# Fused attention and two mixtures: two weight quarters and some split factors of the mixtures are put at earlier places in the instruction lists

## The chip, the cores and the metric

The kernel runs on one core of a Trainium2 chip. The metric is the device time in microseconds of one execution. Five engines work side by side, each through its own list in order: TensorE (PE; its weight loads are shown as PEld), VectorE (DVE), ScalarE (ACT), GpSimd (POOL) and SyncE (SP), which issues loads.

## The reference, cut to what matters

```python
def reference(**kwargs):
    attn_out = _attn_ref(...)                  # 2 x 8 heads, 768 tokens, 64 wide, 16 clusters
    x = np.ascontiguousarray(attn_out.transpose(0, 2, 1, 3)).reshape(B * S, H * D)   # 1536 x 512
    x = _moe_ref(x=x, **moe_kwargs)
    return _moe2_ref(x=x, **moe2_kwargs)

def _attn_ref(q, k, v, centroids):
    # each query and key goes to the centroid with the largest cosine
    mask = q_assign[:, :, :, None] == k_assign[:, :, None, :]
    scores = np.where(mask, scale * np.matmul(q, k.transpose(0, 1, 3, 2)), -1000000000.0)
    ...                                        # softmax of scores
    return np.matmul(attn, v)

def _moe_ref(x, w_in, w_out):                  # w_in 512 x 2048, w_out 2048 x 512
    h = x @ w_in
    return (h * (1.0 / (1.0 + np.exp(-h)))) @ w_out

def _moe2_ref(x, w_gate, w1, w2):              # 8 experts, 512 x 1024 and 1024 x 512
    ...                                        # P: softmax of x @ w_gate, normalised 8 times by rows and columns
    for e in range(E):
        out += P[:, e:e + 1] * (np.maximum(x @ w1[e], 0.0) @ w2[e])
    return out
```

## The kernel before, in words

**Factors.** Every fp32 matrix of a product is split in a high and a low fp32r part: ACT casts the high part, DVE subtracts it and writes the low one. A product is three matmul groups (high by high, high by low, low by high). Names ending in `h` and `l` are such pairs: `vh`/`vl` of the first mixture's w_in, `yh`/`yl` (tiles `yf`) of its x, `woh`/`wol` of w_out, `gh`/`gl` of the activated hidden block; `wfh`/`wfl`, `xfh`/`xfl` and `ah`/`al` of the second mixture's weights, x and hidden block.

**Attention** takes the first 235.5 us. It is a software pipeline over eight pairs of heads; the table `ORDER` gives one pair's steps as `name,offset` (some 27 us a pair), and writes the lists of all engines. The last rows, beyond pair 7, drain it. `ex` is the exponential on ACT, `rec` the reciprocal of its sums on DVE (two steps); POOL scales `p` by it, `T` transposes `p` on PE into `t`, and DVE and ACT copy `t` to `pt` for `av`. `xh` and `xl` split the result and write x sums of its quadrants (`xa` to `xd`).

**Quarters.** Each slice of w_in (even n) or w_out (odd n) is 4 raw quarters, (n, k). `w_raw` loads one on SP's queue; `w_steps` narrows it: `wb` and `w0` on ACT, `w1` to `w4` on DVE, the product `wp0` on POOL and the sum `wp1` on DVE; for w_out `wh` (ACT) and `wp2` (DVE) follow, which give `woh` and `wol`. Four quarters, those of n=0, are loaded by step `wd` in pairs 0 to 3 and narrowed within attention in the pairs behind each load, in the tile `scratch`.

**First mixture** (235.5 to 498.3 us): four slices s of 512 hidden columns. Each is seven products `aproduct` by a scheme of Strassen's kind (order `AORD` 1, 5, 6, 3, 7, 2, 4; called product 0 to 6 by place below, and 4.3 us each), whose factors are x split `yf[p]` and weight factor `mfactor(s, i)`; `aevac` copies the product's banks from PSUM to `h` (ACT) or adds them (DVE), `gsilu`, `ghi` and `glo` activate and split. Then come 12 tiles `ytile` of the second layer, each followed by a sum, `total`, which adds the tile's bank to `acc1` on DVE. A unit u (0 to 18) is one product or one tile: `put(s, u, f, ...)` lays further work into a unit, behind the unit's evacuation or sum and ahead of its matmuls. The lists follow this written order on all engines.

**Second mixture** (from 498.3 us): eight experts in two halves, 16 slices of 14 products. `factor`, `w_sums1`, `w_sums2` make weight factors and sums, `x_factor` and `x_sum` those of x, which is `acc1`. `gate` computes the logits.

The ring of raw tiles and of the narrowed ones:

```python
quarters[n, k][key]()
if key == "wp0":
    m = 4 * (n - 1) + k + 2
    load(1 + m // 4, m % 4)
```

Of the kernel before, what the change touches and what calls it, by code (L numbers as in the profile page):

```python
# [38 lines left out]
def attention_moe_kernel(ctx, tc, kq, vp, cent, w_in, w_out, w_gate, w1, w2, out):  # L39
# [87 lines left out]
    def split(p, src, ks=(0, 1)):  # L127
        hi, lo = yf[p]
        for k in ks:
            nc.scalar.copy(hi[:, k], src[:, k])  # L130
        for k in ks:
            nc.vector.tensor_tensor(out=lo[:, k], in0=src[:, k], in1=r(hi[:, k]), op=ALU.subtract)
# [250 lines left out]
    def five():  # L383
        if 5 not in yf:
            both = scp.tile([P, 2, 2, S], F32R, name="yf5", tag="sc")
            yf[5] = (both[:, 0], both[:, 1])
        return yf[5]

    def five_hi(k):
        nc.scalar.copy(five()[0][:, k], xa[:, k])  # L390

    def five_lo(k):
        nc.vector.tensor_tensor(out=five()[1][:, k], in0=xa[:, k], in1=r(five()[0][:, k]), op=ALU.subtract)
# [936 lines left out]
```

## Time and profile before

| | us |
|---|---|
| median of 3 runs (lowest, highest) | 1474.49 (1474.19, 1475.15) |
| profiled execution | 1473.8 |
| its span | 1472.0 |
| attention ends, first mixture ends | 235.5, 498.3 |

The span runs from the first to the last instruction of the profile, and times of day in the trace count from its start. "Granted clock" is the share of TensorE's full clock (2.4 GHz) that the chip let it have; 0.5 is 1.2 GHz. In a timeline the bracket at the end of a row is the idle time of the engine ahead of it and what ended it.

### The profile page before, as it was taken

The numbers are of one execution on the slowest core, as the hardware profiler recorded it, in microseconds if no ns is written. First come the engines' busy times: TensorE is split into PE (matmuls) and PEld (weight loads), VectorE is DVE, ScalarE is ACT, GpSimd is POOL, SyncE is SP. The second block draws the span as 40 slices with busy tenths as digits, with TensorE's granted clock in tenths as the row PEclk, the third lists the DMA queues.
The fourth block names the chain that finished last, engine by engine and source line by source line (L and its number), as shares of the span: only waits on it lengthen the run. The fifth ranks groups of instructions, "written<-read, shape, count | busy, mean of one in ns | idle before, by whom it ended". The sixth has DMA issues, their size and how long they took to land.

```text
span 1472.0 us, 25066 instructions
## 1 busy us (share of the span) xinstructions
PE 1443.1 (98%) x9784; PEld 1293.4 (88%) x9785; DVE 1092.0 (74%) x1734; ACT 948.6 (64%) x1782; POOL 361.3 (25%) x356
## 2 busy tenths in 40 slices
PE   8999998999999899999999999999999999999998
PEld 5777786788888789999999999999999999999998
DVE  7788887778887598857758668577686675875858
ACT  7777676654646266657667576576675765767654
POOL 6677752121120001111222222120211211202111
PEclk9999999999999999999999999999999999999999
DMA  7665511121222017476697897874947959659476
GB/s 222 179 166 154 140 49 58 58 86 49 67 72 72 1 51 176 68 151 152 119 209 114 161 170 126 163 123 91 203 69 139 149 90 178 105 104 183 83 144 129
DMA packets 136311, 177.48 MB, mean 121 GB/s; under 512 B 6272, under 2 KB 108672, under 8 KB 136192
## 3 DMA queue, kind: packets, MB, share of 16 engines
q0 software_dynamic: 83584, 87.30, 39.0%
q1 hardware_dynamic: 51104, 87.32, 19.7%
q8 instruction: 77, 1.26, 0.4%
q10 hardware_dynamic: 1504, 1.25, 0.3%
q14 instruction: 42, 0.34, 0.1%
HBM read 65.36 MB, written 88.87 MB: 105 GB/s over the span
## 4 chain that ended last, share of the span: by engine, by line
PE 77%; DVE 3%; ACT 2%; issue 0%; DVEq 0%; ACTq 0%
PE b L643 33%; PE a L643 30%; PE y L697 9%; PE l L643 5%; DVE vl L124 1%; DVE h L848 1%; DVE h L669 1%; ACT h L674 0%; ACT gh L679 0%; DVE wfl L851 0%; DVE xfl L851 0%; ACT vh L123 0%; PE gl L975 0%; DVE h L1154 0%; ACT woh L98 0%
## 5 line engine op out<-in xcount | busy, mean ns | idle before, releaser
L643 PE MATMUL b<-wfh,ah 128*128 128x256 f32 x1344 | 381.6, 284 | 1.3 <-ACT ah L1063 1.3
L643 PE MATMUL b<-wfh,al 128*128 128x256 f32 x1344 | 381.3, 284 | 0.7 <-DVE al L1073 0.7
L643 PE MATMUL b<-wfl,ah 128*128 128x256 f32 x1344 | 381.0, 283 | 0.0
L643 PE MATMUL a<-xfl,wfh 128*128 128x512 f32 (+1 forms) x896 | 302.8, 338 | 2.6 <-DVE xfl L851 2.6
L643 PE MATMUL a<-xfh,wfh 128*128 128x512 f32 (+1 forms) x896 | 302.8, 338 | 0.0
L643 PE MATMUL a<-xfh,wfl 128*128 128x512 f32 (+1 forms) x896 | 301.8, 337 | 0.0
L1135 POOL DMA_DIRECT2D out_dram<-acc x87 | 126.2, 1567 | 574.4 <-ACT acc L1126 392.6
L643 PEld LDWEIGHTS b<-wfh,ah 128*128 128x128 f32 x1344 | 258.8, 193 | 1.5 <-ACT ah L1063 1.5
L643 PEld LDWEIGHTS b<-wfh,al 128*128 128x128 f32 x1344 | 258.7, 192 | 1.1 <-DVE al L1073 1.1
L643 PEld LDWEIGHTS b<-wfl,ah 128*128 128x128 f32 x1344 | 258.7, 192 | 0.0
L1126 ACT ACTIVATE acc<-b,Pg 128x256 f32<-128x256 f32 x484 | 186.8, 477 | 21.7 <-issue 20.3
L851 DVE TENSOR_TENSOR al<-h,ah 128x768 fp32r<-128x768 f32 x192 | 177.7, 954 | 30.2 <-ACT ah L1065 29.6
L1065 ACT CAST ah<-h 128x768 fp32r<-128x768 f32 x192 | 160.5, 841 | 50.2 <-PE b L643 23.9
L643 PEld LDWEIGHTS a<-xfl,wfh 128*128 128x128 f32 x896 | 170.5, 190 | 20.9 <-DVE xfl L851 3.4
L643 PEld LDWEIGHTS a<-xfh,wfh 128*128 128x128 f32 x896 | 170.6, 190 | 19.8 <-issue 0.6
L643 PEld LDWEIGHTS a<-xfh,wfl 128*128 128x128 f32 x896 | 170.4, 190 | 18.0
L851 DVE TENSOR_TENSOR wfl<-w0r,wfh 128x512 fp32r<-128x512 f32 x96 | 64.8, 690 | 81.1 <-ACT wfh L936 79.0
L848 DVE TENSOR_TENSOR h<-a,h 128x512 f32<-128x512 f32 x144 | 94.2, 685 | 26.4 <-PE a L643 25.6
L1052 ACT COPY h<-a 128x512 f32<-128x512 f32 x144 | 81.3, 591 | 48.1 <-PE a L643 47.9
L300 ACT ACTIVATE p<-s,m 128x768 f32<-128x768 f32 x96 | 86.8, 905 | 37.4 <-DVE m L291 34.9
L291 DVE TENSOR_REDUCE m<-s 128x1 f32<-128x768 f32 x96 | 89.9, 950 | 15.2 <-PE s L284 14.7
L310 POOL TENSOR_SCALAR p<-p,rec 128x768 f32<-128x768 f32 x96 | 86.9, 918 | 53.1 <-DVE rec L305 44.8
(221 smaller groups left out, 2555.9 us busy)
## 6 DMA issues: line engine op xcount, KB each, us to landing
out_dram<-acc POOLq DMA_DIRECT2D x91, 768.0 KB, 9.3
w0r<-in_w_dram SPq DMA_DIRECT2D x16, 1024.0 KB, 6.9
w1r<-in_w_dram SPq DMA_DIRECT2D x16, 1024.0 KB, 6.8
qk<-qk SPq DMA_DIRECT2D x45, 192.0 KB, 3.6
raw<-in_w_out_dram SPq DMA_DIRECT2D x16, 512.0 KB, 3.4
first_out<-acc POOLq DMA_DIRECT2D x10, 768.0 KB, 10.6
raw<-in_kq_dram SPq DMA_DIRECT2D x16, 384.0 KB, 4.4
raw<-in_w_in_dram SPq DMA_DIRECT2D x12, 512.0 KB, 3.7
```

What stands on the lines that cost most here:

```text
L124: nc.vector.tensor_tensor(out=lo, in0=x, in1=r(hi), op=ALU.subtract)
L291: nc.vector.tensor_reduce(out=m, in_=tiles[i]["s"][:, :S], axis=AX.X, op=ALU.max, negate=True)
L300: nc.scalar.activation(t["p"], t.pop("s")[:, :S], AF.Exp, bias=t.pop("m"), accum_out=chunks[c]["sum"][:, j, 0:1])
L310: nc.gpsimd.tensor_scalar(out=p, in0=p, scalar1=chunks[c]["rec"][:, j : j + 1], scalar2=1.0, op0=ALU.mult, op1=ALU.mult)
L643: nc.tensor.matmul(ps[u][:, cols], lhsT=lf(i, k), rhs=rt(j, k), start=fresh and u not in opened, stop=k == 1 and q == 2, skip_group_check= ...
L697: nc.tensor.matmul(out, lhsT=w[:, k, d * P : (d + 1) * P], rhs=g, start=first, stop=last, skip_group_check=True)
L848: e.tensor_tensor(out=out, in0=in0, in1=in1, op=op)
L851: e.tensor_tensor(out=lo, in0=x, in1=r(hi), op=ALU.subtract)
L1052: act.copy(bank(t, u), ps[u])
L1065: act.copy(hi, x)
L1126: act.mul(t[:, 2 * u + m], z[:, m], g)
L1135: gps.dma_start(out=to, in_=t, accum_op=ALU.add)
```

## The change

- Quarters 0 and 1 of the first w_out slice (n=1) are narrowed within attention too: `wd` and all steps up to `wp1` run for six quarters. Raw tiles are a ring of three, `wr`. `b`, and for w_out `a` too, lie in the raw tile itself (every second 32-bit word); only `u` is a tile apart. The next load is issued when a quarter is finished, for a quarter three ahead (before: at `wp0`, two ahead).
- Splits 5, 6, 7 and 4 of x have tiles in the ring of the query tiles (`qkp`). Split 6 is put into the last rows of attention, `f0` (weight factor 0 of slice 0) is put behind the last `rec`. The tile of `xa` to `xd` shares its place with `acc1`.
- In the first mixture the quarters' steps stand in other units, as the diff shows; split 7 a unit earlier, and `woh` of a slice's last quarter ahead of the silus.
- The second mixture's first weight and x factors are put in the units 11 to 18 of slice 3, between the sums; its loads are issued at unit 7 of that slice.

The sequence of matmuls is the same.

```diff
     yf = {p: x_tiles(p, xpool) for p in (1, 3, 2)}
-    xa, xb, xc, xd = (xap.tile([P, 2, S], F32, name=f"x{c}") for c in "abcd")
+    xs = accp.tile([P, 4, 2, S], F32, name="xs", tag="acc")
+    xa, xb, xc, xd = (xs[:, i] for i in range(4))
+    def x_pair(p):
+        t = qkp.tile([P, 2, 2, S], F32R, name=f"yf{p}", tag="qk")
+        yf[p] = (t[:, 0], t[:, 1])
...
-    def w_steps(n, k, a, b, hi=None, lo=None):
+    def w_steps(n, k, a=None):
         low, high = raws[n, k][..., 0], raws[n, k][..., 1]
-        u, ui, ai = low.bitcast(F32), low, a.bitcast(U32)
+        b, odd = low.bitcast(F32), n % 2
+        if odd:
+            a = high.bitcast(F32)
...
+    for p, x in ((5, xa), (6, xc)):
+        for k in range(2):
+            KINDS[f"h{p}{k}"] = early(x_hi, p, x, k)
+            KINDS[f"l{p}{k}"] = early(x_lo, p, x, k)
...
     for key in ("wb", "w0", "w1", "w2", "w3", "w4", "wp0", "wp1"):
-        KINDS[key] = (wstep(key), 1, 0, 4)
+        KINDS[key] = (wstep(key), 1, 0, 6)
...
-        wp0,-2 T,-1 evD,-3 S,3 evD,-1 lv,2 evA,-2 wp1,-2 sim,1,0 rec,0 lv,1 av,-1 mx,2 ld,5 nrm,0 mx,3 ex,2 nrm,1 ex,3 split,3 S,4 xh,-1 rec,1
+        wp0,-2 T,-1 evD,-3 S,3 evD,-1 lv,2 evA,-2 f0,-1 h60,-1 h61,-1 l60,-1 l61,-1 wp1,-2 sim,1,0 rec,0 lv,1 av,-1 mx,2 ld,5 nrm,0 mx,3 ex,2 nrm,1 ex,3 split,3 S,4 xh,-1 rec,1
...
-        rec,4 w2,-1 av,1 mx,10 castd,5 nrm,8 mx,11 ex,10 nrm,9 ex,11 f0,0
+        rec,4 w2,-1 av,1 mx,10 castd,5 nrm,8 mx,11 ex,10 nrm,9 ex,11 l51,0
...
-            put(s, 0, narrow, n, 0, "wb w0")
-            put(s, 0, split, 6, xc)
-            put(s, 0, narrow, n, 0, "w1 w2 w3 w4 wp0")
-        put(s, 0, narrow, n, 0, "wp1 wh wp2")
-        put(s, 0, sum4)
-        put(s, 0, narrow, n, 1, "wb w0 w1 w2 w3 w4 wp0")
-        put(s, 1, sum3)
-        put(s, 1, narrow, n, 1, "wp1 wh wp2")
-        put(s, 1, narrow, n, 2, "wb w0 w1 w2")
-        if s == 0:
-            put(s, 2, split, 7, xb)
-        put(s, 2, narrow, n, 2, "w3 w4 wp0")
-        put(s, 2, narrow, n, 3, "wb w0")
-        put(s, 2, narrow, n, 2, "wp1 wh wp2")
-        put(s, 3, narrow, n, 3, "w1 w2 w3 w4 wp0")
-        put(s, 4, gsilu, 3)
-        put(s, 4, narrow, n, 3, "wp1 wh wp2")
+            put(s, 0, narrow, n, 0, "wh")
+            put(s, 0, narrow, n, 1, "wh")
+            put(s, 0, narrow, n, 0, "wp2")
+            put(s, 0, sum4)
+            put(s, 0, narrow, n, 1, "wp2")
+            put(s, 0, narrow, n, 2, "wb w0 w1 w2 w3 w4 wp0")
+            put(s, 1, sum3)
+            put(s, 1, split, 7, xb)
+            put(s, 1, narrow, n, 2, "wh wp1 wp2")
+            put(s, 2, narrow, n, 3, "wb w0 w1 w2 w3 w4 wp0")
+            put(s, 3, narrow, n, 3, "wh wp1 wp2")
+        else:
+            put(s, 0, narrow, n, 0, "wh wp1")
...
+            put(s, 3, narrow, n, 3, "wb w0 w1 w2 w3 w4 wp0")
+            put(s, 4, narrow, n, 3, "wh wp1 wp2")
+        put(s, 4, gsilu, 3)
...
+    s = NS1 - 1
+    put(s, 11, factor, 0, nc.vector)
+    put(s, 11, factor, 1, nc.vector)
+    put(s, 12, w_sums1, 0, nc.vector)
+    put(s, 13, w_sums2, 0, nc.vector)
+    put(s, 13, x_factor, 1, (0, 0), (0,))
+    put(s, 14, x_factor, 1, (0, 0), (1,))
+    put(s, 14, factor, 2, nc.vector)
+    put(s, 15, x_factor, 2, (1, 0), (0,))
+    put(s, 15, factor, 3, nc.vector)
+    put(s, 16, x_factor, 2, (1, 0), (1,))
+    put(s, 16, factor, 4, nc.vector)
+    put(s, 17, x_sum, (0, 1), (0, 1), (0, 0), (0,))
+    put(s, 18, x_sum, (0, 1), (0, 1), (0, 0), (1,))
+    put(s, 18, x_factor, 5, (0, 1), (0,))
...
     with tc.manual_schedule(engines={ENG.PE, ENG.DVE, ENG.Activation, ENG.Pool}):
-        w_load(0)
-        w_load(7)
-        factor(0, vec)
-        factor(1, vec)
-        x_factor(1, xblk(0, 0))
-        w_sums1(0, vec)
-        w_sums2(0, vec)
-        x_factor(2, xblk(1, 0))
-        factor(2, vec)
-        factor(3, vec)
-        factor(4, vec)
-        x_sum(xblk(0, 1), xblk(0, 1), xblk(0, 0))
-        x_factor(5, xblk(0, 1))
+        x_factor(5, (0, 1), (1,))
```

DVE's list at the end of attention, before: `m` is the maximum of a score tile, `vl0` the low part of weight factor 0, `rec47` the last reciprocal.

```order
L291 TENSOR_REDUCE m94_3045<-s94_3019 128x1
L291 TENSOR_REDUCE m95_3048<-s95_3025 128x1
L124 TENSOR_TENSOR vl0_3057<-win_85,vh0_3056 128x512
L304 TENSOR_REDUCE rec47_3050<-sum3_166 128x2
L305 RECIPROCAL rec47_3050<-rec47_3050 128x2
L327 COPY pt46_3074<-t138_3062 128x4x128
```

The same place in the changed kernel, where `yf5` and `yf6` are x splits 5 and 6, and `xs` holds the x sums:

```order
L304 TENSOR_REDUCE m94_3075<-s94_3048 128x1
L304 TENSOR_REDUCE m95_3078<-s95_3055 128x1
L402 TENSOR_TENSOR yf5_2954<-xs_84,yf5_2954 128x768
L317 TENSOR_REDUCE rec47_3080<-sum3_165 128x2
L318 RECIPROCAL rec47_3080<-rec47_3080 128x2
L340 COPY pt46_3101<-t138_3089 128x4x128
L387 TENSOR_TENSOR yl2_83<-av22_3062,yh2_82 128x256
L394 TENSOR_TENSOR xs_84<-av22_3062,xs_84 128x256
L340 COPY pt47_3128<-t141_3110 128x4x128
L139 TENSOR_TENSOR vl1_3190<-win_85,vh1_3189 128x512
L340 COPY pt47_3128<-t143_3123 128x4x128
L139 TENSOR_TENSOR vl0_3133<-win_85,vh0_3132 128x512
```

The two steps of `rec47` stand ahead of `vl0`, which is now the last of these rows, and the first `pt` copies stand between.

DVE's list at the start of the first mixture, before, from factor 1 (`vl1`); `raw1_0` is the raw tile of quarter (1, 0), `a1_0` and `b1_0` its parts.

```order
L124 TENSOR_TENSOR vl1_3167<-win_85,vh1_3166 128x512
L132 TENSOR_TENSOR yl6_3152<-xc_83,yh6_3151 128x768 x2
L90 TENSOR_SCALAR raw1_0_3160<-raw1_0_3160 128x512
L91 TENSOR_SCALAR raw1_0_3160<-raw1_0_3160 128x512
L92 SCALAR_TENSOR_TENSOR a1_0_3170<-raw1_0_3160 128x512
L93 TENSOR_SCALAR raw1_0_3160<-a1_0_3170 128x512
L95 TENSOR_TENSOR b1_0_3171<-a1_0_3170,b1_0_3171 128x512
L99 TENSOR_TENSOR wol_3159<-b1_0_3171,woh_3158 128x512
L115 TENSOR_TENSOR win_85<-win_85,wsum_86 128x2x256
L90 TENSOR_SCALAR raw1_1_3162<-raw1_1_3162 128x512
```

In the changed kernel, from split 6 to factor 2 (`vl2`); `wr1_0` is the ring's tile of quarter (1, 0), `u1_2` the tile apart of quarter (1, 2):

```order
L402 TENSOR_TENSOR yf6_3136<-xs_84,yf6_3136 128x768 x2
L387 TENSOR_TENSOR yl2_83<-av23_3141,yh2_82 128x256
L394 TENSOR_TENSOR xs_84<-av23_3141,xs_84 128x256
L114 TENSOR_TENSOR wol_3186<-wr1_0_2004,woh_3185 128x512
L130 TENSOR_TENSOR win_85<-win_85,wsum_86 128x2x256
L114 TENSOR_TENSOR wol_3186<-wr1_1_2374,woh_3185 128x512
L107 TENSOR_SCALAR u1_2_3203<-u1_2_3203 128x512
L108 TENSOR_SCALAR u1_2_3203<-u1_2_3203 128x512
L109 SCALAR_TENSOR_TENSOR wr1_2_2739<-wr1_2_2739,u1_2_3203 128x512
L110 TENSOR_SCALAR u1_2_3203<-wr1_2_2739 128x512
L139 TENSOR_TENSOR vl2_3238<-wsum_86,vh2_3237 128x512
```

The narrowing of quarter (1, 0) and split 6 have left this place; the low parts of two quarters stand beside each other, and four steps of quarter (1, 2) are ahead of factor 2.

DVE's list around the last sums of slice 3, before: `y3_10` and `y3_11` are the last two tiles, `w0r0` the second mixture's first raw weights, `ws0` a sum of them.

```order
L720 TENSOR_TENSOR acc1_3480<-y3_10_5278,acc1_3480 128x512
L720 TENSOR_TENSOR acc1_3480<-y3_11_5292,acc1_3480 128x512
L851 TENSOR_TENSOR wfl0_5364<-w0r0_5359,wfh0_5363 128x512
L851 TENSOR_TENSOR wfl1_5368<-w0r0_5359,wfh1_5367 128x512
L851 TENSOR_TENSOR xfl1_5372<-acc1_3480,xfh1_5371 128x768 x2
L848 TENSOR_TENSOR w0r0_5359<-w0r0_5359 128x2x256
L848 TENSOR_TENSOR ws0_5377<-w0r0_5359 128x512
L848 TENSOR_TENSOR w0r0_5359<-w0r0_5359,ws0_5377 128x2x256 x2
L851 TENSOR_TENSOR xfl2_5383<-acc1_3480,xfh2_5382 128x768 x2
L851 TENSOR_TENSOR wfl2_5389<-ws0_5377,wfh2_5388 128x512
```

In the changed kernel, from the sum of tile 8 on; `h21` takes the next x sum:

```order
L750 TENSOR_TENSOR wfl3_5283<-w0r0_5111,wfh3_5282 128x512
L729 TENSOR_TENSOR acc1_3475<-y3_8_5286,acc1_3475 128x512
L750 TENSOR_TENSOR xfl2_5279<-acc1_3475,xfh2_5278 128x768
L750 TENSOR_TENSOR wfl4_5303<-w0r0_5111,wfh4_5302 128x512
L729 TENSOR_TENSOR acc1_3475<-y3_9_5306,acc1_3475 128x512
L747 TENSOR_TENSOR acc1_3475<-acc1_3475 128x768
L729 TENSOR_TENSOR acc1_3475<-y3_10_5321,acc1_3475 128x512
L747 TENSOR_TENSOR acc1_3475<-acc1_3475 128x768
L750 TENSOR_TENSOR xfl5_5337<-acc1_3475,xfh5_5336 128x768 x2
L729 TENSOR_TENSOR acc1_3475<-y3_11_5340,acc1_3475 128x512
L747 TENSOR_TENSOR h21_0_5389<-acc1_3475 128x768 x2
L750 TENSOR_TENSOR xfl6_5393<-h21_0_5389,xfh6_5392 128x768 x2
```

Weight factors 0 to 2 and x factor 1 stand further up, and the rest of this work stands between the sums of tiles 7 to 11; behind the last sum stands the x sum `h21`.

## Rows read from the trace of the kernel before

**Rows 1.** The page: engines' busy us, share of the span, instructions.
```profile
PE 1443.1 (98%) x9784; PEld 1293.4 (88%) x9785; DVE 1092.0 (74%) x1734; ACT 948.6 (64%) x1782; POOL 361.3 (25%) x356
```

**Rows 2.** Stretches: length, busy of PE, PEld, DVE, ACT, POOL, then granted clock.
```profile
88.90:116.30 27.40, 27.38 (x213) 21.31 (x211) 23.23 (x47) 20.09 (x42) 20.40 (x22) 1.00 0.64 166
143.70:171.10 27.40, 26.86 (x211) 20.98 (x209) 23.46 (x49) 19.21 (x40) 20.24 (x22) 1.00 0.57 159
...
235.50:276.60 41.10, 34.26 (x169) 28.53 (x169) 33.24 (x53) 28.88 (x46) 5.91 (x4) 0.88 0.17 52
...
498.30:545.00 46.70, 41.08 (x231) 32.98 (x231) 44.35 (x59) 24.80 (x39) 0.70 (x3) 0.93 0.08 24
```

**Rows 3.** PE's waits, 200 to 545 us: total, times, longest.
```profile
PE l L643 <- DVE h L669: 4.6, 4, 3.1
PE l L643 <- DVE vl L124: 3.1, 1, 3.1
PE a L643 <- DVE xfl L851: 2.6, 1, 2.6
PE t L319 <- POOL p L310: 1.8, 1, 1.8
PE b L643 <- ACT ah L1063: 1.3, 1, 1.3
PE gl L975 <- DVE acc L848: 1.2, 1, 1.2
PE l L643 <- ACT h L665: 0.7, 1, 0.7
PE b L643 <- DVE al L1073: 0.5, 1, 0.5
```

**Rows 4.** Timeline, end of attention: start, us, instruction, idle before.
```profile
228.01 0.69 DVE L124 TENSOR_TENSOR vl<-win,vh 128x512 fp32r<-128x512 f32 x1 [1.65 <-ACT vh L123]
...
228.62 0.15 DVE L304 TENSOR_REDUCE rec<-sum 128x2 f32<-128x4 f32 x1
...
230.09 1.21 PE L319 MATMUL t<-ident,p 128*128 128x128 f32 x6 [1.84 <-POOL p L310]
```

**Rows 5.** Stretches behind PE's waits, and two others; columns as in rows 2.
```profile
248.62:253.90 5.28, 5.28 (x15) 4.31 (x16) 5.14 (x8) 4.88 (x9) 1.11 (x1) 0.51 0.34 99
270.78:274.50 3.72, 3.72 (x9) 2.91 (x10) 3.72 (x6) 2.64 (x4) 0.00 (x0) 0.54 0.02 4
501.35:506.70 5.35, 5.35 (x20) 4.35 (x21) 5.28 (x8) 1.76 (x3) 0.00 (x0) 0.68 0.00 0
540.09:544.00 3.91, 3.91 (x20) 3.91 (x21) 3.91 (x5) 2.26 (x5) 0.00 (x0) 0.56 0.01 4
230.09:233.00 2.91, 2.58 (x16) 1.67 (x18) 1.51 (x3) 0.59 (x1) 0.83 (x1) 1.00 0.79 318
490.00:498.30 8.30, 8.30 (x38) 6.90 (x37) 2.07 (x3) 0.00 (x0) 0.00 (x0) 1.00 0.00 0
420.00:440.00 20.00, 20.00 (x104) 17.14 (x103) 16.78 (x30) 5.84 (x10) 4.16 (x3) 1.00 0.31 102
```

**Rows 6.** DVE's timeline, first products of slice 0.
```profile
238.49 1.83 DVE L132 TENSOR_TENSOR yl<-xc,yh 128x768 fp32r<-128x768 f32 x2 [1.15 <-ACT yh L130]
...
241.88 0.43 DVE L93 TENSOR_SCALAR raw<-a 128x512 uint32<-128x512 uint32 x1
243.90 0.69 DVE L95 TENSOR_TENSOR b<-a,b 128x512 f32<-128x512 f32 x1 [1.59 <-POOL b L94]
```

**Rows 7.** Timeline ahead of product 6 of slice 0.
```profile
258.99 0.62 ACT L123 CAST vh<-win 128x512 fp32r<-128x512 f32 x1 [0.94 <-PE l L643]
...
261.36 0.69 DVE L124 TENSOR_TENSOR vl<-win,vh 128x512 fp32r<-128x512 f32 x1
...
264.77 0.60 ACT L98 CAST woh<-a 128x512 fp32r<-128x512 f32 x1
```

**Rows 8.** Line 92, third step of a quarter: min/median/max ns by tile.
```profile
L92 DVE SCALAR_TENSOR_TENSOR a<-raw x16: 682/692/694, 241.2 to 451.2; 128x512 uint32<-128x512 uint32 x16
```

More of the change, by code (lines that the diff above doesn't have):

```diff
@@ L125, in mfactor, with split @@
         wfac[s, i] = (hi, lo)
[L127 to L132, printed above, removed]
+    def split(p, src):
+        for part in (x_hi, x_lo):
+            for k in range(2):
+                part(p, src, k)
     actx = ExitStack()
@@ L381, in xlo, with x_hi, x_lo @@
             v(out=xd[at], in0=ps, in1=xc[at], op=ALU.subtract)
[L383 to L393, printed above, removed]
+    def x_hi(p, src, k):
+        if p not in yf:
+            x_pair(p)
+        nc.scalar.copy(yf[p][0][:, k], src[:, k])
+    def x_lo(p, src, k):
+        nc.vector.tensor_tensor(out=yf[p][1][:, k], in0=src[:, k], in1=r(yf[p][0][:, k]), op=ALU.subtract)
     def wd(k):
-        w_raw(0, k, scratch[:, k % 2].bitcast(U32))
+        w_raw(*divmod(k, 4))
     def wstep(key):
@@ L727, in attention_moe_kernel @@
     quarters = {}
-    def load(n, k):
-        if n < 2 * NS1:
-            w_raw(n, k, rp.tile([P, 2 * FB], F32, name=f"raw{n}_{k}", tag="wraw").bitcast(U32))
-    def narrow(n, k, keys):
-        if (n, k) not in quarters:
-            if n % 2:
-                a = rp.tile([P, 1, FB], F32, name=f"a{n}_{k}", tag="na")
-                b = rp.tile([P, 1, FB], F32, name=f"b{n}_{k}", tag="nb", bufs=3)
-                quarters[n, k] = w_steps(n, k, a, b, wo_h[:, k : k + 1], wo_l[:, k : k + 1])
-            else:
-                quarters[n, k] = w_steps(n, k, win[:, :, k * P : (k + 1) * P], rp.tile([P, 4, P], F32, name=f"b{n}_{k}", tag="nb", bufs=3))
-        for key in keys.split():
-            quarters[n, k][key]()
-            if key == "wp0":
-                m = 4 * (n - 1) + k + 2
-                load(1 + m // 4, m % 4)
@@ L1164, in h_s43, with narrow @@
             tt(vec, hb[s, to][:, k], hb[s, c][:, k], hb[s, "11"][:, k], ALU.subtract)
+    def narrow(n, k, keys):
+        if (n, k) not in quarters:
+            quarters[n, k] = steps.pop(k + 4, None) if n == 1 else None
+            quarters[n, k] = quarters[n, k] or w_steps(n, k, None if n % 2 else win[:, :, k * P : (k + 1) * P])
+        for key in keys.split():
+            quarters[n, k][key](*((wo_h[:, k : k + 1], wo_l[:, k : k + 1]) if key in ("wh", "wp2") else ()))
+            m = 4 * n + k + 3
+            if key == ("wp1", "wp2")[n % 2] and 6 < m < 8 * NS1:
+                w_raw(m // 4, m % 4)
```

269 lines of the change are left out of this document (141 added, 128 removed).

## The prediction

> **What bounds the kernel now.** I read the page's first part, then the stretches of the span, then TensorE's waits, and the instructions around the longest of these. TensorE is busy 98% of the span [rows 1]. The change keeps the sequence of its matmuls, so it can only win back time in which TensorE waits or runs at a low clock. The stretches say where that is [rows 2]: an attention pair loses 0.02 us of 27.40, but the first 41.1 us of the first mixture keep TensorE busy for 34.26 with a mean granted clock of 0.88, and the first 46.7 us of the second mixture for 41.08 at 0.93. The waits name the causes [rows 3]. All those of these two places end on VectorE (DVE) or ScalarE (ACT), so DVE's and ACT's lists there are what the sum is made from. In all, some 16 us of waits stand between 200 and 545 us, and the low clock behind them is the other part.
>
> That part shows in five stretches [rows 5]. Three that begin with a matmul after a wait of 3.1, 3.1 or 2.6 us have a granted clock of 0.51, 0.54 and 0.68: mostly the 1.2 GHz level. At 2.4 GHz the same work would be shorter by the missing share: 5.28 x 0.49 = 2.6 us, 3.72 x 0.46 = 1.7, 5.35 x 0.32 = 1.7. The fourth, after 1.3 and 0.5, lost 3.91 x 0.44 = 1.7. The fifth, after 1.84 us, kept clock 1.00.
>
> **The change part by part.**
>
> a. *Two more quarters in attention, and x factors of splits 5 and 6.* Each quarter adds five DVE steps (0.43 or 0.69 us each, [rows 6, 8]), two on ACT and one on POOL to one of the pairs 5 to 7. A pair with a quarter and no x sums loses 0.02, one with a quarter and x sums 27.40 - 26.86 = 0.54 [rows 2]. The later pairs carry x sums. Bounds: 0 (all hidden in DVE's idle 4 us of a pair, 27.40 - 23.46) and 2 x 0.54 = 1.1. I take the middle, **+0.5**.
>
> b. *The last `rec`.* It stands behind `vl0` on DVE, which waits for ACT's cast `vh0`; TensorE then waits 1.84 for POOL's scaling by this `rec` [rows 4]. Now `f0` is put later, and `rec` stands ahead of `vl0`. Its input, the last `ex` on ACT, ends ahead of that cast, which takes 0.6 and which `vl0` follows at 228.01: so it was there by about 227.5, and `rec` began at 228.62, 1.1 us later. Bounds 0 and the whole 1.84. **-1.1**.
>
> c. *Product 2 of slice 0.* TensorE waits 0.7 for `h` and 3.1 for `vl2` [rows 3]. The `vl2` stood on DVE behind split 6 (1.83), the whole narrowing of quarter 0 with a wait of 1.59 for POOL's `b` in its middle, quarter 0's low part, a sum and four steps of quarter 1 [rows 6]. Now it stands behind the low parts of two quarters, the sum and four steps of quarter 2. Gone are 1.83, 1.59, `b`'s 0.69 and four steps, three of 0.43 and one of 0.69, 2.0; one low part of 0.69 is new: 5.4 us less, more than the 3.8 waited. So both waits go, and with them the low clock: 0.7 + 3.1 + 2.6 = **-6.4**. Bounds: -3.8 (the clock falls anyway) and -6.4.
>
> d. *Product 6 of slice 0.* TensorE waits 3.1 for `h` of product 3's column [rows 3]: the longest of the four. Two of its parts can be seen [rows 7]. DVE's `vl` started 261.36 though the cast it needs ended at 258.99 + 0.62 = 259.61, so it was 1.75 late, 0.2 of that ordinary hand-over: 1.55 of backlog, the narrowing of quarter 3. And ACT's `woh` of quarter 3 stood between the silus and `gh`: 0.5 of its 0.60, for the next instruction starts before it ends. In the changed order the narrowing of quarter 3 stands one product earlier and `woh` ahead of the silus. 3.1 - 1.55 - 0.5 = 1.0 stays, since the rest (the evacuations, silu, `gh`, split 4, `vl6`, each behind the other) is as before: **-2.1**. Bounds -0.5 and -3.1. The clock's 1.7 (second row of [rows 5]): the wait left is shorter than the 1.84 that was followed by full clock, but hardly shorter than the 1.3 and 0.5 that was followed by 1.2 GHz. The first of these followed nearly unbroken work, and product 6 will now too, so I take **-1.7**; bounds 0 and -1.7.
>
> The Trainium skill, "TensorE: Matmul & The Clock Gate", Part 1, What's actually happening, says that the throttled clock is the default and that activity releases it. By that rule the preceding business counts, which would keep the clock up here and leave 1454; by the row of 540.09 alone it would fall, and the time be 1456. The trace shows both outcomes, so it does not settle this.
>
> e. *Slices 1 to 3.* Their waits at the same place are 4.6 - 3.1 = 1.5 in three [rows 3]. `woh` ahead of the silus takes 0.5 from each; the narrowing of quarter 3, a unit later than before, gives 0.2 back: 3 x 0.3 = **-0.9**. Bounds -1.5 and +0.5.
>
> f. *The entry of the second mixture.* All of DVE's work for the first factors stood behind the last sum: TensorE waited 2.6 for `xfl` and 1.2 for the logits' x sum, with 1.7 of low clock [rows 3, 5]. What is moved between the sums is nine operations of 512 columns at 0.69 and seven of 768 at 0.91 (a pair of them 1.83, [rows 6]): 12.6 us. The cover: in the last 8.30 us DVE is busy 2.07, three sums of 0.69 [rows 5], so 2.1 us of every tile are free; eight tiles give 16.6. The sums need not come late, and the tiles' banks are freed in time: each step put behind a sum is shorter than 2.1 us or waits on ACT, which is idle there. So 2.6 + 1.2 + 1.7 = **-5.5**. DVE was busy 44.35 of 46.70 in this stretch [rows 2], so its work is 12 us ahead when the first `ah` is due: the 1.3 + 0.5 and the 1.7 of clock go but for 0.3 of ACT's own chain, an estimate, **-3.2**. If the factors come too late (a cast of ACT queued behind another tile's sum), only the 2.6 goes; at most -9.0.
>
> The two loads that are issued later, the weights' ring of three and the gate's weights land well before their use, at a cost of nothing; if a quarter's load is late, the wait for it is one load's remaining flight, within the bound of c.
>
> **Sum.** 0.5 - 1.1 - 6.4 - 2.1 - 1.7 - 0.9 - 5.5 - 3.2 = -20.4. The profiled execution took 1473.8 (span 1472.0 and 1.8 around it), so 1453.4; it was 0.7 under the median of 1474.49, so **1454.1 us** as the runs are timed, 1.4% less.
>
> **Rivals.**
>
> A. *Product 6 still stalls in full.* DVE's list binds there all the same, because the factors, the narrowing of quarter 3 and two low parts are still ahead of its `vl`; for it: `woh` and quarter 3 were shifted by one product only. Against: 1.55 of the delay is one named backlog. The 3.1 and the low clock stay: 1454.1 + 3.8 = 1457.9. Chance 0.15.
>
> B. *Attention pays.* The added quarters stall transposes or score tiles in two pairs in full and the last `rec` gains nothing (the scaling on POOL still waits for something else): +0.6 + 1.1 = 1455.8. For it: the 0.54 in a pair of both kinds. Against: DVE idles there 4 us. Chance 0.08.
>
> C. *The entry does not gain:* the change does not do what it says there. Each engine takes its list in order, so one step that waits for an ACT cast of another step, or a weight load, holds the next sum, the tile's bank and then TensorE. Of the 8.7 only the 2.6 would remain, or not even that: 1454.1 + 6.1 to + 8.7, **1460 to 1463**. Against: 4 us of spare cover. Chance 0.08.
>
> D. *Slower than before: in-place narrowing.* The steps now read and write `a` and `b` as every second word of the raw tile, in four DVE steps a quarter (0.69, 0.43, 0.69, 0.69 = 2.5 us, [rows 6, 8]) and POOL's product. If such operands doubled the price on DVE, a slice's four second-layer quarters would add 10 us to some 30 us of products where DVE has 4.8 free (3.2 idle of 20, [rows 5]): 5.2 in each of three slices and 5.0 in slice 0, 20.6 in all: 1474.7, no change. If POOL's 1.5 (5.91 in four, [rows 2]) doubles too, DVE waits for it another 1.5 in each slice: 1481. So it decides from a factor of two on. Against it: the step that already reads every second word takes 0.69 [rows 8], as does a plain one [rows 4]. Chance 0.03.
>
> **How the numbers follow.** The likeliest, the forecast with small deviations, holds 0.66; its own range is 1450.5 to 1457.5, from the bounds of a to e taken two at a time. Rivals A to C lie above it; below it there are only e's bound and b's (1452). The range that leaves out no more than 2 in 10 is **1450 to 1463**. About 0.2% (2.9 us) is what a measurement of this kernel can tell from no change. All but D end faster by more than that; 0.03 I add for a mechanism that none of these names. So faster 0.94, within 0.2% 0.02, slower 0.04.
>
> **What would show it.** The 0.7 and 3.1 at about 245 and 248 gone, and the matmuls there at clock 1.00; a wait near 1.0 before the sixth product; waits for `p` in the tail of 0.7 or so; no `a` matmul waiting for `xfl` at the entry, and the last sums still ending about 2 us before their banks are asked for. The prediction is wrong if new waits stand in the y tiles of the last slice, if the first product of slice 0 waits for an x factor, or if DVE's steps on every second word take more than 0.7.

## The result and the profile after

The changed kernel took 1452.06 us (median of 4 runs, 1451.20 to 1452.94), the kernel before 1474.82 beside it: ratio 0.9846, 95% interval 0.9829 to 0.9863. The forecast was 1454.1, its range 1450 to 1463. The profiled execution has a span of 1450.6 us, 21.4 less than before.

The page of the changed kernel (engines' busy us, share of the span, instructions; it answers to [rows 1]):

```profile
span 1450.6 us, 25095 instructions
...
PE 1436.4 (99%) x9784; PEld 1288.6 (89%) x9785; DVE 1089.7 (75%) x1734; ACT 944.6 (65%) x1782; POOL 361.3 (25%) x356
```

TensorE is busy 6.7 us less with the same matmuls, so part of the gain lies inside its busy time: matmuls at the full clock that had run at the low one. The rest is idle time. TensorE's waits between 200 and 545 us, total, times and longest, against [rows 3]:

```profile
PE t L332 <- POOL p L323: 1.1, 2, 0.7
PE l L652 <- DVE h L678: 1.1, 1, 1.1
PE col L910 <- DVE cs L905: 0.6, 1, 0.6
...
```

The waits for `vl`, `xfl`, `ah`, the logits' `acc` and ACT's `h` are gone, that for DVE's `h` is 1.1 once instead of 4.6 in four (in slices 1 to 3 TensorE still idles 0.14 to 0.15 there, too little for this view). A new one of 0.6 waits for a step of the gate, `col`. The two waits that stay, the one in attention's tail and the one at product 6 of slice 0, in TensorE's timeline:

```profile
230.44 1.87 PE L332 MATMUL t<-ident,p 128*128 128x128 f32 x12 [0.71 <-POOL p L323]
...
262.24 0.70 PE L652 MATMUL l<-yf,vh 128*128 128x512 f32 x2 [1.08 <-DVE h L678]
```

Stretches of the changed kernel, columns as in [rows 2], the granted clock third from the end:

```profile
235.82:266.51 30.69, 29.61 (x170) 25.86 (x169) 24.38 (x38) 22.68 (x37) 3.36 (x2) 1.00 0.22 69
262.24:266.00 3.76, 3.76 (x20) 3.25 (x21) 3.76 (x6) 2.68 (x4) 0.00 (x0) 1.00 0.00 0
487.40:508.50 21.10, 21.10 (x135) 16.65 (x134) 17.93 (x24) 11.76 (x20) 0.40 (x1) 1.00 0.17 51
```

Slice 0's products take 30.69 us at clock 1.00, where [rows 2, 5] showed 0.88 and stretches of 0.51 and 0.54. The entry of the second mixture has no idle time at all (21.10 of 21.10).

To see where each microsecond came from, the span is cut at instructions that both kernels have. These rows of TensorE's timeline open slice 0, its first y tile, the second mixture, and its first `b` product. Before:

```profile
235.48 0.50 PE L643 MATMUL l<-yh,vh 128*128 128x512 f32 x1
...
276.63 0.40 PE L697 MATMUL y<-gh,woh 128*128 128x512 f32 x1
...
498.34 0.39 PE L643 MATMUL a<-xfh,wfh 128*128 128x512 f32 x1
...
539.09 0.39 PE L643 MATMUL b<-wfh,ah 128*128 128x256 f32 x1 [1.27 <-ACT ah L1063]
```

After:

```profile
235.82 0.50 PE L652 MATMUL l<-yh,vh 128*128 128x512 f32 x1
...
266.51 0.40 PE L706 MATMUL y<-gh,woh 128*128 128x512 f32 x1
...
487.40 0.39 PE L652 MATMUL a<-xfh,wfh 128*128 128x512 f32 x1
...
519.83 0.28 PE L652 MATMUL b<-wfh,ah 128*128 128x256 f32 x1
```

With the first transposes that wait for POOL (at 29 to 31 us) and the last output group that POOL issues as further marks, the stages of all kernels that ran are these. Each number is the difference of two marks, in the profiled execution. The letters are those of the prediction's parts.

| kernel | start-up | attention (a, b) | slice 0 products (c, d) | to the second mixture (e) | entry to first `b` (f) | to last output (f) | end | span |
|---|---|---|---|---|---|---|---|---|
| before | 29.11 | 206.37 | 41.15 | 221.71 | 40.75 | 916.11 | 16.80 | 1472.0 |
| changed | 30.18 | 205.64 | 30.69 | 220.89 | 32.43 | 914.54 | 16.23 | 1450.6 |
| e1_entry_back | 29.30 | 205.60 | 30.68 | 220.93 | 40.72 | 915.29 | 16.88 | 1459.4 |
| e2_quarters_back | 30.17 | 204.79 | 38.79 | 220.91 | 32.43 | 914.57 | 15.74 | 1457.4 |
| e3_split6_back | 29.27 | 205.54 | 30.67 | 220.91 | 32.43 | 914.58 | 17.30 | 1450.7 |
| e4_f0_ahead | 29.41 | 207.45 | 30.64 | 220.86 | 32.43 | 914.56 | 15.75 | 1451.1 |
| e5_pad1 | 30.11 | 205.50 | 31.27 | 220.89 | 32.43 | 914.56 | 16.34 | 1451.1 |
| e5_pad3 | 29.18 | 205.54 | 34.30 | 220.92 | 32.43 | 914.56 | 16.47 | 1453.4 |
| e6_split4_earlier | 31.30 | 205.60 | 29.30 | 220.93 | 32.43 | 914.56 | 16.88 | 1451.0 |
| e7_woh_back | 30.13 | 205.52 | 31.16 | 222.62 | 32.43 | 914.54 | 16.90 | 1453.3 |
| e8_one_quarter | 29.20 | 205.01 | 35.67 | 220.89 | 32.43 | 914.56 | 15.84 | 1453.6 |

The middle stages repeat to about 0.1 us where nothing in them was edited; the start-up and the end scatter by some 2 us. So an edit is read from its stage, and a span alone says little below 2 us. From before to changed the stages give +1.07, -0.73, -10.46, -0.82, -8.32, -1.57 and -0.57, in all -21.4.

### The profile page after: what moved, and what is told of

Its sections match the earlier page's. It is cut to its first block, busy times and chain, and to the rows that moved or that the text cites. A ratio compares the mean times of both kernels' runs of the same rounds, so it can differ in the third digit from the quotient of the medians.

```text
span 1450.6 us, 25095 instructions
## 1 busy us (share of the span) xinstructions
PE 1436.4 (99%) x9784; PEld 1288.6 (89%) x9785; DVE 1089.7 (75%) x1734; ACT 944.6 (65%) x1782; POOL 361.3 (25%) x356
## 4 chain that ended last, share of the span: by engine, by line
PE 89%; DVE 6%; ACT 3%; issue 1%; DMA 0%; POOL 0%; DVEq 0%; ACTq 0%; POOLq 0%
PE b L652 32%; PE a L652 31%; PE y L706 9%; PE l L652 4%; PE av L354 4%; PE t L332 3%; PE s L295 2%; PE s L297 2%; DVE m L304 1%; DVE al L750 1%; ACT p L313 1%; DVE h L678 1%; DVE pt L340 1%; ACT h L674 1%; DVE h L747 0%
## 5 line engine op out<-in xcount | busy, mean ns | idle before, releaser
L1022 ACT ACTIVATE acc<-b,Pg 128x256 f32<-128x256 f32 x484 | 186.4, 476 | 21.8 <-issue 20.4
L747 DVE TENSOR_TENSOR h<-a,h 128x512 f32<-128x512 f32 x144 | 94.5, 685 | 29.4 <-PE a L652 28.5
```

What stands on the lines that cost most here:

```text
L747: e.tensor_tensor(out=out, in0=in0, in1=in1, op=op)
L1022: act.mul(t[:, 2 * u + m], z[:, m], g)
```

## The experiments

All are the changed kernel with one edit.

**The entry undone (e1_entry_back).** The factors stand behind the last sum again.

```diff
-    put(s, 11, factor, 0, nc.vector)
...
-    put(s, 18, x_factor, 5, (0, 1), (0,))
...
         total(NS1 - 1, 11)
+        factor(0, vec)
+        factor(1, vec)
+        x_factor(1, (0, 0))
+        w_sums1(0, vec)
+        w_sums2(0, vec)
+        x_factor(2, (1, 0))
+        factor(2, vec)
+        factor(3, vec)
+        factor(4, vec)
+        x_sum((0, 1), (0, 1), (0, 0))
+        x_factor(5, (0, 1), (0,))
```

> The changed kernel with one part undone: the second mixture's first weight and x factors stand behind the last sum of slice 3 again (their loads stay at unit 7). Theory, by the two traces: from the first matmul of the second mixture to the first b product the stretch goes from 32.4 us back to about 40.8, and about 2.1 us more are lost behind it: +10.5 in all, span about 1461. Rival 1, the forecast's own sum for this part: +8.7, span about 1459.3. Rival 2, that only the wait for the first xfl was saved: +2.6, about 1453.2.

Measured: 1461.15 us (median of 4), ratio to before 0.9914 (0.9899 to 0.9928); the stage goes from 32.43 to 40.72, as it was before (40.75). TensorE's waits there, from its timeline:

```profile
489.53 0.80 PE L652 MATMUL a<-xfl,wfh 128*128 128x512 f32 x1 [2.62 <-DVE xfl L750]
...
497.47 1.71 PE L871 MATMUL gl<-acc,wgr 128*32 128x384 f32 x12 [1.44 <-DVE acc L747]
...
527.23 0.38 PE L652 MATMUL b<-wfh,ah 128*128 128x256 f32 x1 [1.20 <-ACT ah L959]
```

and the stretches behind the first and the third:

```profile
489.50:495.00 5.50, 5.47 (x23) 4.62 (x23) 5.43 (x8) 1.77 (x3) 0.00 (x0) 0.70 0.00 0
527.20:532.00 4.80, 4.28 (x33) 4.08 (x34) 4.79 (x6) 3.15 (x6) 0.00 (x0) 1.00 0.02 3
```

So the three waits of the kernel before come back in size and place, and with them the low clock behind the first (0.70). Behind the third, 1.20 and another 0.5, the clock stayed at 1.00; in the kernel before it fell behind the same wait (fourth row of [rows 5]). The part behind the first `b` product is 0.75 longer than in the changed kernel here, and was 1.57 longer before. So undoing the entry costs 8.29 + 0.75 = 9.0: near the first rival, the forecast's 8.7, and less than the 10.5 expected. The kernel before lost 9.9 there, the difference being the low clock of its first `b` products. The rival of 2.6 is out.

**The two quarters back in slice 0 (e2_quarters_back).**

```diff
-        KINDS[key] = (wstep(key), 1, 0, 6)
+        KINDS[key] = (wstep(key), 1, 0, 4)
...
-            put(s, 0, narrow, n, 0, "wh")
-            put(s, 0, narrow, n, 1, "wh")
-            put(s, 0, narrow, n, 0, "wp2")
+            put(s, 0, narrow, n, 0, "wb w0 w1 w2 w3 w4 wp0 wh wp1 wp2")
             put(s, 0, sum4)
-            put(s, 0, narrow, n, 1, "wp2")
-            put(s, 0, narrow, n, 2, "wb w0 w1 w2 w3 w4 wp0")
+            put(s, 0, narrow, n, 1, "wb w0 w1 w2 w3 w4 wp0")
             put(s, 1, sum3)
+            put(s, 1, narrow, n, 1, "wh wp1 wp2")
+            put(s, 1, narrow, n, 2, "wb w0 w1 w2")
             put(s, 1, split, 7, xb)
-            put(s, 1, narrow, n, 2, "wh wp1 wp2")
+            put(s, 2, narrow, n, 2, "w3 w4 wp0")
+            put(s, 2, narrow, n, 2, "wh wp1 wp2")
```

> The changed kernel with one part undone: quarters (1,0) and (1,1) are narrowed in unit 0 of slice 0 again (loaded in attention as now; split 6 stays in attention's tail). Theory: attention ends up to 1 us earlier (the two quarters cost it about that), but vl2 comes behind 4 us more of DVE work and a wait for POOL, so a wait of 1 to 3 us with some 2 of low clock returns at product 2: span +2 to +5, 1452.5 to 1455.5. Rival, split 6 alone had made product 2 late: no wait returns, span -1, 1449.6.

Measured: 1459.45 us (median of 4), ratio to before 0.9904 (0.9888 to 0.9921), 7.4 over the changed kernel and more than expected. Attention is 0.85 shorter, slice 0 8.10 longer. TensorE's timeline in slice 0:

```profile
249.82 0.39 PE L652 MATMUL l<-yh,vl 128*128 128x256 f32 x1 [1.48 <-DVE vl L139]
...
256.45 0.50 PE L652 MATMUL l<-yf,vl 128*128 128x512 f32 x1 [1.98 <-DVE vl L139]
...
267.90 0.69 PE L652 MATMUL l<-yf,vh 128*128 128x512 f32 x2 [3.05 <-DVE h L678]
```

No wait returned at product 2, where the theory put it: the three stand at products 3, 4 and 6. Granted clock behind each, third number from the end:

```profile
249.82:254.00 4.18, 4.18 (x23) 3.69 (x24) 2.55 (x5) 3.60 (x7) 1.33 (x1) 1.00 0.00 0
256.45:260.50 4.05, 4.04 (x23) 3.46 (x23) 2.80 (x5) 1.39 (x2) 1.11 (x1) 1.00 0.17 50
267.90:271.60 3.70, 3.69 (x11) 2.97 (x12) 3.70 (x6) 2.61 (x4) 0.00 (x0) 0.66 0.02 4
271.60:274.00 2.40, 2.40 (x16) 2.16 (x16) 2.40 (x4) 2.40 (x4) 0.00 (x0) 0.81 0.00 0
```

Full clock behind 1.48 and 1.98, low behind 3.05, worth 3.70 x 0.34 + 2.40 x 0.19 = 1.7. How the last wait comes about is seen on ACT and DVE, ACT first:

```profile
255.95 0.61 ACT L138 CAST vh<-win 128x512 fp32r<-128x512 f32 x1
```

```profile
257.60 0.69 DVE L112 TENSOR_TENSOR wr<-wr 128x512 f32<-128x512 f32 x1 [1.20 <-POOL wr L111]
...
259.01 0.68 DVE L139 TENSOR_TENSOR vl<-win,vh 128x512 fp32r<-128x512 f32 x1
259.61 1.88 DVE L678 TENSOR_TENSOR h<-l,h 128x512 f32<-128x512 f32 x3
```

The cast that factor 5 needs ends at 256.56, but DVE starts its low part at 259.01, because the narrowing of quarter 3 is ahead of it, with a wait for POOL in it. The first evacuation behind it starts at 259.61, and product 6 begins 8.29 us later, at 267.90. In the changed kernel the same chain runs from 253.94 to 262.24, 8.30 us. So with the row behind it as it is, product 6 hangs on the time at which DVE is through with its list, and the backlog of two quarters reaches it across five products.

**Split 6 back in slice 0 (e3_split6_back).**

```diff
-        ... f0,-1 h60,-1 h61,-1 l60,-1 l61,-1 wp1,-2 ...
+        ... f0,-1 wp1,-2 ...
             put(s, 0, mfactor, 0, 1)
+            put(s, 0, split, 6, xc)
```

> The changed kernel with one part undone: x split 6 stands at the start of unit 0 of slice 0 again, and not in attention's last rows. Theory: vl2 was ready some 3 us before its product, more than the 1.8 of this split, so nothing returns: span within 0.4 of 1450.6. Rival, this split is what had made product 2 late: a wait of 1 or more at product 2 and low clock behind it, +2 to +4.

Measured: 1452.44 us in one run, no wait in slice 0 but the one of 1.08, and its stage 30.67 as against 30.69. The theory holds; with the quarters gone, this split has cover where it stood before.

**`f0` ahead of the last `rec` again (e4_f0_ahead).**

```diff
-        ... f0,-1 h60,-1 ...
+        ... h60,-1 ...
-        ... ex,11 l51,0
+        ... ex,11 f0,0 l51,0
```

> The changed kernel with one part undone: weight factor 0 (f0) is put ahead of the last rec again, so the last rec stands behind vl0 on DVE. Theory: the wait of the last transposes for p goes from 0.71 back to about 1.8, attention ends 1.1 later, span 1451.7. Rival, POOL's scaling waited for something else: the wait stays near 0.7.

Measured: 1452.90 us in one run; attention 207.45, about 1.9 longer than the 205.5 to 205.6 of the kernels that leave it as changed. TensorE's wait, and the stretch behind it:

```profile
231.47 1.86 PE L332 MATMUL t<-ident,p 128*128 128x128 f32 x12 [2.69 <-POOL p L323]
```

```profile
231.47:235.00 3.53, 3.20 (x22) 2.09 (x24) 2.69 (x5) 2.01 (x3) 0.83 (x1) 1.00 0.00 0
```

The wait is 2.69, not 1.8: in the changed list a low part of split 5, 0.95 us, also stands ahead of `rec`, and here it is pushed back behind `vl0`, with `rec` behind it. So the edit is worth 1.9 where it stands now. The clock stayed at 1.00 behind 2.69 us. The rival is out.

**The wait at product 6 made longer (e5_pad1, e5_pad3)** by operations of 512 columns on DVE ahead of factor 6, whose result nothing uses (one, and in a second kernel three):

```diff
             put(s, 4, split, 4, xd)
+            for _ in range(1):
+                put(s, 4, lambda: nc.vector.tensor_tensor(out=xa[:, 0, :FB], in0=xc[:, 0, :FB], in1=xc[:, 1, :FB], op=ALU.add))
```

> The changed kernel with one extra, useless DVE operation of 512 columns (0.69 us) ahead of weight factor 6 in slice 0; its result is used by nothing. Theory: product 6 hangs on the chain behind DVE's list (8.3 us from the first evacuation of product 3's column), so its wait goes from 1.08 to about 1.7; the clock stays at 1.00 behind it, as it did behind 1.48, 1.98 and 2.69 us elsewhere: span +0.6. Rival, as behind the 1.3 and 0.5 of the kernel before, the clock falls and 1.7 more are lost.

> The same with three such operations: the wait goes to about 2.9. Theory: the waits that were always followed by the low clock were 2.6 and longer at this place, so the clock falls and 1.7 are lost on top: span +3.5. Rival, 2.69 in attention's tail was followed by full clock, so 2.9 is too: span +1.8.

Measured with one: 1452.89 us in one run; the wait and the stretch around it:

```profile
262.62 0.70 PE L652 MATMUL l<-yf,vh 128*128 128x512 f32 x2 [1.69 <-DVE h L678]
```

```profile
262.00:266.00 4.00, 3.38 (x17) 2.92 (x18) 4.00 (x7) 2.29 (x4) 0.00 (x0) 1.00 0.00 0
```

With three: 1455.20 in one run:

```profile
263.19 0.72 PE L652 MATMUL l<-yf,vh 128*128 128x512 f32 x2 [3.14 <-DVE h L678]
```

```profile
263.50:267.50 4.00, 4.00 (x12) 3.18 (x11) 4.00 (x7) 3.23 (x5) 0.00 (x0) 0.57 0.00 0
```

The stage grows by 0.58 and by 3.61. Of the second, 2.06 is wait and 1.55 low clock (clock 0.57). So at this matmul, behind the same work, 1.69 us is followed by full clock and 3.14 by a stretch mostly at 1.2 GHz, in one run each. Both theories hold, both rivals are out.

**Split 4's casts a unit earlier (e6_split4_earlier).** This aims at the 1.08 that is left.

```diff
         if s == 0:
-            put(s, 4, split, 4, xd)
+            for k in range(2):
+                put(s, 3, x_hi, 4, xd, k)
+            for k in range(2):
+                put(s, 4, x_lo, 4, xd, k)
```

> The changed kernel with the casts of x split 4 one unit earlier (unit 3, ahead of the cast of factor 5), so that silu, gh, split 4 and factor 6 no longer stand in one row ahead of product 6. Theory: that row sets the 1.08 us wait; 1.6 of it goes, so the wait goes to 0: span 1449.5, about 1 us faster than the changed kernel, which timing can hardly tell. Rival, DVE's evacuations hold product 6 anyway: the wait stays near 1.

Measured: 1451.73 us (median of 5), ratio to before 0.9844 (0.9831 to 0.9858). TensorE in the stretch of slice 0 is never idle:

```profile
235.00:270.00 35.00, 35.00 (x203) 30.06 (x199) 29.96 (x44) 27.66 (x45) 3.33 (x2) 1.00 0.20 61
```

The stage falls by 1.39 to 29.30, the wait is 0. So the 1.08 hung on ACT's row as well as on DVE's list. The theory holds in the trace; the runs cannot tell this kernel from the changed one. Its span is not shorter because its profiled execution had the longest start-up of all, 31.30, and an end 0.65 longer.

**`woh` of the last quarter behind the silus again (e7_woh_back)**, in all slices:

```diff
-            put(s, 3, narrow, n, 3, "wh wp1 wp2")
...
-            put(s, 4, narrow, n, 3, "wh wp1 wp2")
         put(s, 4, gsilu, 3)
+        put(s, 4, narrow, n, 3, "wp1 wh wp2")
         put(s, 4, ghi, 3)
```

> The changed kernel with one part undone: in all four slices the last quarter's woh stands behind the silus on ACT again (in slice 0 with its wp1 and wp2, a unit later). Theory: ACT's row silu, woh, gh, split 4, factor 6 gets 0.5 longer, DVE's ahead of product 6 does not: the wait goes from 1.08 to about 1.6, the clock stays 1.00, slices 1 to 3 wait 0.4 each again: span +0.5 to +1.7. Rival, DVE's two moved steps delay product 6 as well: the wait goes to 3.

Measured: 1455.10 us in one run. TensorE's waits in slice 0, and in slice 1 for the two that follow alike:

```profile
262.56 0.70 PE L652 MATMUL l<-yf,vh 128*128 128x512 f32 x2 [1.59 <-DVE h L678]
...
325.75 0.70 PE L652 MATMUL l<-yf,vh 128*128 128x512 f32 x2 [0.72 <-DVE h L678]
```

1.59 in slice 0, with full clock; 0.72 in each of the slices 1 to 3. Slice 0 grows by 0.47, the three others by 1.73 together: 2.2, somewhat more than expected at most. The rival of 3 is out: `wp1` and `wp2` cost nothing here.

**Only one quarter in attention (e8_one_quarter).** `KINDS` goes to 5, and quarter 1 is narrowed in units 0 and 1 of slice 0, with the steps of quarter 2 where the experiment on both had them.

```diff
-        KINDS[key] = (wstep(key), 1, 0, 6)
+        KINDS[key] = (wstep(key), 1, 0, 5)
...
+            put(s, 0, narrow, n, 1, "wb w0 w1 w2 w3 w4 wp0")
             put(s, 1, sum3)
+            put(s, 1, narrow, n, 1, "wh wp1 wp2")
```

> The changed kernel with only quarter (1,0) narrowed in attention; quarter (1,1) is narrowed in units 0 and 1 of slice 0 again. Theory: DVE's backlog builds over the whole of slice 0: half of what both quarters cost (6.8 us of span) less the 3 us of slack ahead of factor 2, so a wait of 0 to 1.5 at products 3 to 5 and one of 1 to 2.5 at product 6, span +1 to +3; attention 0.4 shorter. Rival, the slack takes one quarter whole: span within 0.5 of 1450.6.

Measured: 1455.39 us in one run, span +3.0. The waits, and the clock behind the second:

```profile
252.58 0.50 PE L652 MATMUL l<-yf,vl 128*128 128x512 f32 x1 [0.94 <-DVE vl L139]
...
264.03 0.90 PE L652 MATMUL l<-yf,vh 128*128 128x512 f32 x2 [3.05 <-DVE h L678]
```

```profile
264.03:268.00 3.97, 3.97 (x11) 3.12 (x12) 3.97 (x7) 2.88 (x4) 0.00 (x0) 0.57 0.02 4
```

Attention is 0.6 shorter, slice 0 4.98 longer: 2.9 of wait, 1.7 of low clock (0.57 over 3.97 us), and 0.4 in smaller steps. The small wait is within the forecast, the one at product 6 is above it: it is the same 3.05 as with two quarters. In both kernels TensorE already waits for `vl` at product 4, at 256.45 and 252.58, and product 6 begins 11.45 us later. So once TensorE waits for the list there, more backlog makes that wait longer (0.94 with one quarter, 1.98 with two) and leaves the later one as it is.

## Why the prediction was right, step by step

The forecast's sum was -20.4, the traces give -21.4, of which +0.5 are start-up and end, where nothing was changed. So the stages that were changed give -21.9. The mechanisms named came out, each with its wait; that the sum is this near is in part luck, since errors of both signs in a, b and f partly cancel. (The chances given add up to 1.03, 0.03 too much; nothing rests on it.)

**a, two quarters in attention**, +0.5 forecast. Without them attention is 0.85 shorter, with one of them 0.2 longer than that. Within the bounds, and small beside what they save. Split 6 adds nothing that shows (attention 205.54 without it, 205.50 to 205.64 with it).

**b, the last `rec`**, -1.1. The wait for `p` went from 1.84 to 0.71. a and b together: -0.73 by the stage, -0.6 by the sum. With a at 0.85 that leaves about -1.6 for b, split 5 included, which no run takes apart: both terms were too small, and they partly cancel. Undone in the changed kernel the edit costs 1.9, since a further step now stands there: a price read from the old list is a price in the old list.

**c, product 2**, -6.4. The waits of 0.7 and 3.1 and the low clock went, as the count of DVE's list said. DVE's timeline after, around factors 2 and 5:

```profile
238.21 0.68 DVE L114 TENSOR_TENSOR wol<-wr,woh 128x512 fp32r<-128x512 f32 x1
...
240.85 0.69 DVE L139 TENSOR_TENSOR vl<-wsum,vh 128x512 fp32r<-128x512 f32 x1
...
253.33 0.69 DVE L139 TENSOR_TENSOR vl<-win,vh 128x512 fp32r<-128x512 f32 x1 [0.42 <-ACT vh L138]
```

`vl` of factor 2 starts at 240.85, behind a low part at 238.21 and four steps, where it started at 247.88 before: 7.0 earlier, 5.4 by the count. Up to the wait ahead of product 6 the slice is 6.9 shorter.

**d, product 6**, -2.1 and -1.7 of clock. 1.08 stayed, forecast 1.0, at clock 1.00 (second of the changed kernel's stretches above): 2.0 of wait and 1.6 of clock are gone. c and d together: -10.46 by the stage, -10.2 by the sum. The two pieces found in the trace were real: 0.5 for `woh` (1.59 with it back), and DVE's backlog. One thing the forecast did not say: c and d are not independent. The backlog is cleared by moving the quarters, not by putting quarter 3 a unit earlier; with quarter 1 or both back, the wait at product 6 is 3.05 in spite of that. Without the backlog `vl` of factor 5 starts at 253.33, at once behind its cast, which ends at 253.30.

**e, slices 1 to 3**, -0.9; -0.82 by the stage. The waits of 1.5 in three fall to 0.14 to 0.15 each, where 0.2 was forecast to stay; with `woh` behind the silus again the three slices are 1.73 longer, so that edit gives 0.58 a slice where 0.5 was forecast. The waits fall by 1.1 in all and the stage by 0.82: 0.12 of the difference lies in the y tiles of four slices (32.99 us each for 32.96), the rest is open.

**f, the entry**, -8.7; -9.9 by the two stages. This is the term that was mis-sized. The forecast counted 1.2 for the logits, the wait shown. The rows are those of the logits' matmuls, before:

```profile
507.23 0.84 PE L975 MATMUL gl<-acc,wgr 128*32 128x384 f32 x4
509.29 1.71 PE L975 MATMUL gl<-acc,wgr 128*32 128x384 f32 x12 [1.22 <-DVE acc L848]
```

and after:

```profile
491.68 1.50 PE L871 MATMUL gl<-acc,wgr 128*32 128x384 f32 x16
```

Sixteen of them take 1.50 us in one piece. Before, there is a second stop inside the row of 12, which the row does not show; the weight loads do:

```profile
510.15 0.14 PEld L975 LDWEIGHTS gl<-acc,wgr 128*32 128x32 f32 x4 [0.71 <-DVE acc L848]
```

The starts in the trace tell what the stops cost. After, the sixteen start in four groups of four, some 0.33 apart, and the next product starts at 493.11, 1.43 behind the first. Before, the two halves of the sum, which end at 509.23 and 510.10, split two of these groups: two start at 507.23, two at 507.57, four at 509.29, four at 509.63, two at 510.15, two at 510.50, and the next product at 510.92, 3.69 behind the first. Of the difference of 2.26 the first stop is 1.4, the second 0.2, and two more steps of 0.34 are the rest. So the logits were worth 2.3, not 1.2.

Cut at these marks, the -9.9 are 4.6 up to the logits (2.6 + 1.7 were forecast), 2.3 in them (1.2), 1.45 from there to the first `b` product (1.3), and 2.25 from it to the gate's transposes `plog`, at 545.77 before and 524.26 after (0.5 + 1.7). Then 0.7 is given back, by a cost that the forecast did not have: the new wait for the gate's step `col`.

```profile
543.39 0.39 PE L910 MATMUL col<-cs,ones 128*128 128x8 f32 x2 [0.56 <-DVE cs L905]
```

Between the first two of these steps lie 5.27 us (538.12 to 543.39), 4.58 before (559.63 to 564.21). The kernel with the entry undone has the same 5.27, and its `b` products kept full clock. So the low clock of the first `b` products before was priced at 1.7 but was worth some 0.8 in the end: 1.5 there (from the first `b` product to `plog` are 6.68 us before, 5.16 with the entry undone, 4.43 in the changed kernel), of which TensorE now waits 0.7 for the gate. The 0.3 kept for ACT's own chain at the first `b` product was not needed.

**The clock.** The Trainium skill, "TensorE: Matmul & The Clock Gate", Part 1, What's actually happening, says that activity releases the throttle, as the prediction has it for d. The runs agree with what the prediction made of this at product 6: full clock behind waits of 1.08, 1.59 and 1.69 us; behind 3.05 and 3.14 there it fell. It does not settle the entry: behind 1.2 and 0.5 the clock fell in the kernel before and did not in the kernel with the entry undone.

**The rivals.** A (product 6 stalls in full) would have held with one quarter fewer in attention. B is out by the stage of attention. C is out: no y tile of slice 3 waited (TensorE is busy 32.99 of the 32.99 us from 454.41 to 487.40). D is out by the changed kernel's rows of the steps that now write or read every second word (min, median and max ns):

```profile
L109 DVE SCALAR_TENSOR_TENSOR wr<-wr,u x16: 680/686/693, 173.0 to 442.1; 128x512 uint32<-128x512 uint32 x16
...
L112 DVE TENSOR_TENSOR wr<-wr x16: 679/682/805, 180.0 to 445.6; 128x512 f32<-128x512 f32 x16
```

That is 0.68 to 0.69 us, as in [rows 8]. POOL's product takes 1.32 in both kernels.

## What to carry to other kernels

Count the list of the engine that is late, not the wait alone: here a wait of 3 us behind a list that loses 5.4 us went entirely, and a backlog put back into that list showed up later, at products 3, 4 and 6. Cut the span at instructions that both kernels have; here stages repeat to 0.1 us where spans scatter by 2. A row that groups several instructions can hide a second stop, and that they start two at a time and not four: compare its time from start to next start with the same group elsewhere. Look behind the place that gets faster for work that was in time only because TensorE was slower, as the gate's step was here.

## What the runs showed of the hardware

Behind a wait, TensorE's clock stayed at 2.4 GHz after 1.08, 1.48, 1.59, 1.69, 1.98 and 2.69 us, and fell to 1.2 GHz for a part of the stretch behind 2.62 (the entry), 3.05 (twice), 3.14, and 3.1 (twice in the kernel before, [rows 3, 5]). That 2.69 at the end of attention kept it (one run) and 2.62 at the entry lost it, in both kernels that had that wait, shows that the length of the wait alone doesn't decide. The wait of 1.2 and 0.5 at the first `b` product had either outcome, with the same sequence of matmuls, in one profile each.

The first 30 us also have several outcomes, 29.1 to 29.4, 30.1 to 30.2 and once 31.3. In the longer ones the first matmuls of the cluster scores take nearly twice as long. First the changed kernel, then the one with the entry undone:

```profile
5.66 1.51 PE L197 MATMUL sim<-raw,chl 128*32 128x384 f32 x8 [0.18 <-POOL cst L509]
```

```profile
5.60 0.85 PE L197 MATMUL sim<-raw,chl 128*32 128x384 f32 x8 [0.39 <-POOL cst L509]
```

Both have a granted clock of 1.00 in the profile there, so the column doesn't show what differs, and why is open. The kernel with 31.3 has the same 1.51, so something else is longer there too. The end scatters by 1.6 us, from the last output group that POOL issues to the end of the span.
